# A new order of the boot in a two-layer memory-transformer kernel

## The chip, the cores and the metric

The kernel runs on one core of a Trainium2 chip. The metric is the device time of one execution in microseconds, the median of several runs. A core has five engines with instruction streams of their own: TensorE (PE, matrix products), VectorE (DVE), ScalarE (ACT), GpSimd (POOL) and SyncE (SP, which here only issues transfers). Transfers are started by an instruction on SP or POOL and then run by themselves.

## The reference

The input x is 2048 rows of 512 values in bfloat16. The reference does the same two steps twice, with the same weights:

```
x = x + A(layernorm(x))      # attention over segments, with a memory
x = x + B(layernorm(x))      # (sigmoid(x Wg) * (x Wu)) Wd, 512 -> 1792 -> 512
```

A cuts the 2048 rows into 64 segments of 32. For each segment, 8 memory rows are put ahead of the 32 rows, and 32 heads of width 128 attend over these 40 rows:

```
h = concat([mem, xs])                 # 40 x 512
q, k, v = h Wq, h Wk, h Wv            # 32 heads x 128
p = softmax(where(mask, q k^T * scale, -1e9))
o = (p v) Wo                          # 40 x 512
mem = o[:8]; out = o[8:]
```

The memory rows that come out of a segment go into the next, so the 64 segments of one layer are a chain; a segment can't begin its attention ahead of the end of the one before.

## The kernel before, in words

**Stages.** The first layer runs segment after segment, and the second follows six segments behind, so that most of the 70 steps (`NSTEPS`) work on one segment of each layer at once. A step (`emit_step`, L777) goes through five groups of heads, g0 to g4. For each part of a group it projects q and k (L874, from `hT`, the transposed normalised rows, with `wq_sb` and `wk_sb`), copies them from PSUM into `qku`, forms the scores (L910), adds the mask and takes the maximum on VectorE (L924 and after), the exponentials on ScalarE (L934), transposes the probabilities (L956), multiplies them with V (L982, `vsb`) and applies Wo (L1001). After every four segments a feed-forward block of 128 rows runs (`ffn`, L1056), whose weights POOL fetches anew every time (L1095, L1096, L1120).

**The boot.** V of the 32 plain rows of a segment doesn't depend on the memory, so V of the first layer is made in bulk in the boot: `v_group` and `v_pass` (L708, L631; matmuls L641) normalise 16 blocks of x, multiply them with `wv_sb`, and store the rows in a buffer in device memory, `scr`. `v_half` (L668) and `v_strip` (L698) do so for the parts that steps need first, with the matmuls at L768. From `scr` each step's V rows come back into `vsb` (L1230). Nine tiles of the feed-forward weights (`wd`, `wg`, `wu`) serve as staging for these stores until the first feed-forward block needs them; a staging tile is free once its store has landed. The strips have a single staging tile of their own, `sst`. Wv, Wq, Wk and Wo are loaded once (`load_weights`, L511, loads at L519): Wv in 8 loads of 4 heads, Wq and Wk in 6 loads each, of 3, 6 or 7 heads (384, 768 and 896 KB), Wo in 12.

**What sets the order.** The code names tasks with what they read and write (`Planner.add`): 13976 in all. The order in which the tasks are issued is not computed but stored: `SEQUENCE` (L53) is a compressed list with the place of each task among those still left, and behind it one bit for each task that may go on either of two engines (copies on ScalarE or VectorE, some transfers on SP or POOL). `plan` (L247) unpacks it. Each engine runs its tasks in this order, and a task waits for the tasks it depends on, so a task that waits holds up all behind it on its engine. Which PSUM bank or staging tile a task gets also follows from the order.

`replay` (L266) goes through the order once with the constants of L182 to L192 (rate of the transfers, times to landing and so on) and gives each task a planned start. The planned starts have two uses in the program. A large weight load on POOL is made to wait for a certain matmul, the last one that is planned to be done by the load's planned time:

```
w = (tk.nb + self.FIX) / self.CP
own = max(own, a) + w
t = max(t, own - self.LEAD[e] - self.ROOM)
tk.pace = pes[k].idx if k >= 0 else None
```

And `warm` (L340) puts matmuls without a purpose of their own (L1220) into planned pauses of TensorE.

## Time and profile before

| | |
|---|---|
| median of 3 runs | 1744.15 us |
| lowest and highest | 1743.08 and 1746.82 us |
| profiled execution | 1744.94 us |
| its span in the trace | 1743.2 us |
| TensorE busy in the span | 1718.3 us (99%) |
| VectorE, ScalarE, POOL busy | 1253.1, 1146.2, 872.6 us |
| bytes moved by transfers | 273.41 MB, 157 GB/s over the span |

A row of the timeline has the start, the time taken, engine, line and operation, the tile written and the tile read, and in the last bracket how long the engine had been idle before it and what ended the wait. A window row has the busy time of each engine in a stretch (with the number of instructions), the granted clock of TensorE as a share of full speed, the busy share of the 16 transfer engines and the rate. SPq and POOLq stand for the issuing of transfers on SP and POOL. A row of waits has the total, the number of times and the longest.

### The profile page before, as it was taken

The page shows a single profiled execution, that of the slowest core. Times are in us where ns is not written, and L with a number is a line of the kernel's source. Part 1 is how long each engine was busy: PE and PEld are TensorE (multiplying, and loading weights), DVE is VectorE, ACT ScalarE, POOL GpSimd, SP SyncE. Part 2 cuts the span into 40 slices and gives each one's busy share as a digit, 9 for nine tenths or more (in the row PEclk, how much of TensorE's full clock was granted, in tenths as well). Part 3 has the DMA queues.
Part 4 walks back from the last instruction along what each step waited for, and adds up shares of the span by engine and source line. Part 5 has one row for each costly group of instructions (what it writes and reads, how often), then busy time and mean ns, then how long its engine had stood idle before and what let it go on. Part 6 is the DMA issues. An engine that isn't in the chain of part 4 may idle for free.

```text
span 1743.2 us, 91561 instructions
## 1 busy us (share of the span) xinstructions
PE 1718.3 (99%) x38936; PEld 1492.0 (86%) x39151; DVE 1253.1 (72%) x4178; ACT 1146.2 (66%) x3149; POOL 872.6 (50%) x1401
## 2 busy tenths in 40 slices
PE   9899999999999999999999999999999999999999
PEld 4688789889898988989898888988888898988887
DVE  5677687677776766776677778776777876776766
ACT  4576777566666766676666666666666666666665
POOL 7535255545544564545455454645545454554443
PEclk9999999999999999999999999999999999999999
DMA  9835364655545464646455464545645454554544
GB/s 323 289 112 162 88 175 138 176 148 157 152 129 174 130 186 122 176 115 185 141 152 173 131 178 121 169 131 166 172 133 171 132 160 124 164 158 133 157 145 124
DMA packets 145155, 273.41 MB, mean 157 GB/s; under 512 B 39838, under 2 KB 86114, under 8 KB 144746
## 3 DMA queue, kind: packets, MB, share of 16 engines
q0 software_dynamic: 74144, 201.30, 39.7%
q1 hardware_dynamic: 70602, 66.25, 12.8%
q8 instruction: 307, 5.03, 1.2%
q14 instruction: 102, 0.84, 0.2%
HBM read 221.78 MB, written 27.07 MB: 143 GB/s over the span
## 4 chain that ended last, share of the span: by engine, by line
PE 91%; DVE 3%; DMA 2%; issue 1%; ACT 1%; SPq 0%; POOL 0%; DVEq 0%; POOLq 0%; ACTq 0%
PE bank L874 32%; PE bank L1001 17%; PE bank L1103 11%; PE bank L768 7%; PE bank L641 7%; PE bank L910 4%; PE bank L982 4%; PE bank L1126 4%; PE bank L956 2%; PE bank L601 1%; DVE st L924 1%; DMA wq_sb<-in_A_Wq_dram 1%; PE bank L1220 1%; DMA wk_sb<-in_A_Wk_dram 1%; PE bank L1071 0%
## 5 line engine op out<-in xcount | busy, mean ns | idle before, releaser
L874 PE MATMUL bank<-hT,wk_sb 128*128 128x80 bf16 (+3 forms) x8960 | 616.9, 198 | 3.5 <-DMA wk_sb<-in_A_Wk_dram 3.2
L874 PE MATMUL bank<-hT,wq_sb 128*128 128x80 bf16 (+3 forms) x8960 | 617.0, 198 | 2.2 <-DVE hT L1014 0.3
L1234 ACT CAST qku<-bank 128x480 bf16<-128x480 f32 (+3 forms) x770 | 384.1, 507 | 206.8 <-PE bank L874 179.2
L874 PEld LDWEIGHTS <-wq_sb 128*128 128x128 bf16 x8960 | 454.4, 99 | 31.8 <-issue 15.8
L874 PEld LDWEIGHTS <-wk_sb 128*128 128x128 bf16 x8960 | 447.5, 99 | 3.5 <-DMA wk_sb<-in_A_Wk_dram 3.5
L1001 PE MATMUL bank<-otsb,wo_sb 128*128 128x80 bf16 (+1 forms) x8960 | 355.7, 198 | 0.5
L924 DVE TENSOR_TENSOR st<-bank,cst 40x240 f32<-40x240 f32 (+3 forms) x768 | 280.9, 368 | 97.8 <-PE bank L910 81.8
L1001 PEld LDWEIGHTS <-wo_sb 128*128 128x128 bf16 x8960 | 333.3, 99 | 10.8 <-issue 0.6
L1230 POOL DMA_DIRECT2D vsb<-sst x360 | 182.3, 510 | 193.7 <-ACT sst L1234 86.9
L1234 ACT CAST otsb<-bank 128x480 bf16<-128x480 f32 (+3 forms) x420 | 200.4, 483 | 80.8 <-PE bank L982 47.1
L1120 POOL DMA_DIRECT2D wd<-in_B_w_down_dram x217 | 157.2, 725 | 136.3 <-PE bank L910 36.5
L1095 POOL DMA_DIRECT2D wg<-in_B_w_gate_dram x217 | 165.9, 765 | 118.3 <-PE bank L1103 53.2
L1096 POOL DMA_DIRECT2D wu<-in_B_w_up_dram x217 | 166.2, 767 | 106.0 <-PE bank L1103 36.2
L934 ACT ACTIVATE st<-st 80x240 f32<-80x240 f32 (+3 forms) x420 | 160.2, 383 | 73.1 <-DVE st L931 69.3
L1226 ACT ACTIVATE ptsb<-bank,small 120x160 bf16<-120x160 bf16 (+3 forms) x442 | 163.1, 387 | 16.0 <-PE bank L956 9.8
L1103 PE MATMUL bank<-xnT,wg 128*128 128x128 bf16 (+2 forms) x1784 | 171.4, 218 | 0.4
L936 DVE TENSOR_REDUCE small<-st 80x6 f32<-80x240 f32 (+3 forms) x420 | 151.7, 363 | 27.2 <-ACT st L934 25.0
L1103 PE MATMUL bank<-xnT,wu 128*128 128x128 bf16 (+2 forms) x1784 | 171.1, 218 | 0.0
L1230 POOL DMA_DIRECT2D vsb<-scr x197 | 104.4, 531 | 116.0 <-PE bank L982 57.0
L910 PE MATMUL bank<-qku 128*128 128x80 bf16 (+1 forms) x2240 | 159.3, 198 | 2.2 <-ACT qku L1234 0.9
L931 DVE TENSOR_TENSOR st<-st,small 80x240 f32<-80x240 f32 (+3 forms) x420 | 155.5, 371 | 7.8
L945 DVE TENSOR_TENSOR pb<-st,small 80x240 bf16<-80x240 f32 (+3 forms) x420 | 154.5, 370 | 7.4
(108 smaller groups left out, 2563.7 us busy)
## 6 DMA issues: line engine op xcount, KB each, us to landing
wg<-in_B_w_gate_dram POOLq DMA_DIRECT2D x220, 256.0 KB, 4.0
wu<-in_B_w_up_dram POOLq DMA_DIRECT2D x220, 256.0 KB, 4.1
wd<-in_B_w_down_dram POOLq DMA_DIRECT2D x220, 256.0 KB, 3.9
scr<-vst SPq DMA_DIRECT2D x90, 96.0 KB
vsb<-scr SPq DMA_DIRECT2D x120, 66.0 KB
vsb<-scr POOLq DMA_DIRECT2D x110, 66.0 KB, 3.2
vsb<-sst SPq DMA_DIRECT2D x189, 32.0 KB
vsb<-sst POOLq DMA_DIRECT2D x159, 32.0 KB, 2.5
```

The source lines that it names most:

```text
L874: nc.tensor.matmul(o_ap, lhsT=W[:, c, h * P:(h + 1) * P], rhs=mv(c), start=(c == 0), stop=(c == DC - 1))
L910: nc.tensor.matmul(s_all(SB)[:, w0 + i, :], lhsT=fview(qku[:, i, 0, 0:1], [(1, P)]), rhs=qku[:, i, 1, 0:ncol], start=True, stop=True)
L924: pl.add("DVE", dve_ns(n, True), lambda gsz=gsz, hs=hs, st=st, SB=SB, pj_=pj_, npj_=npj_, mk=mk, idx=idx: nc.vector.tensor_tensor(out=st[p ...
L934: pl.add("ACT", act_ns(n), lambda hs=hs, st=st: nc.scalar.activation(out=st[pr, hs], in_=st[pr, hs], func=ACTF.Exp, scale=self.scale), r=s ...
L1001: nc.tensor.matmul(WB[:, c * ncol:(c + 1) * ncol], lhsT=self.wo[:, h, c * P:(c + 1) * P], rhs=otsb[:, hl, 0:ncol], start=(h == 0 and c == ...
L1095: pl.add("POOL", 760, lambda wg=wg, fs=fs: nc.gpsimd.dma_start(out=wg[:], in_=self.wgv[:, :, fs]), r=[("wo", self.H - 1)], w=[gk] + bt, la ...
L1096: pl.add("POOL", 760, lambda wu=wu, fs=fs: nc.gpsimd.dma_start(out=wu[:], in_=self.wuv[:, :, fs]), r=[("wo", self.H - 1)], w=[uk] + bt, la ...
L1103: nc.tensor.matmul(gu[:, 2 * i + k, 0:n], lhsT=W[:, c, i * P:(i + 1) * P], rhs=xnT[:, c, rw], start=(c == 0), stop=(c == DC - 1))
L1120: pl.add("POOL", 760, lambda wd=wd, ip=ip: nc.gpsimd.dma_start(out=wd[:], in_=self.wdv[:, 2 * ip:2 * ip + 2, :]), w=[dk] + (["boot"] if se ...
L1226: nc.scalar.activation(out=dst, in_=src, func=ACTF.Copy, scale=by)
L1230: {"SP": nc.sync, "POOL": nc.gpsimd}[tk.on].dma_start(out=got[1], in_=got[2])
L1234: nc.scalar.copy(out=dst, in_=src)
```

## The change

`SEQUENCE` is replaced, and four constants of `replay` get other values: BUS from 330 to 322, TAIL from 1850 to 1900, STEAL from 1.2 to 0.5 and FIX from 12400 to 6000. The tasks themselves, their number and what they depend on stay as they are.

Unpacked, the two orders differ as follows. TensorE's tasks are in another order from the 8th to the 459th, which ended before at about 205 us; all later ones are the same. On ScalarE and VectorE some 400 and 440 tasks from the boot on are affected, on POOL the first 178 and on SP the first 180. 176 tasks change engine: on balance ScalarE gives 10 copies to VectorE, and SP and POOL exchange the same number of transfers. Some of the moves, with places counted from 0 in the order of the engine, and KB counted as the planner weighs the transfers up to and with the one named:

| | before | after |
|---|---|---|
| SP: Wo heads 16-18 (384 KB) | place 21 | place 55 |
| SP: Wq heads 3-8 | place 51 | place 39 |
| SP: Wk heads 9-15 | place 34, 9029 KB | place 41, 11296 KB |
| SP: Wk heads 25-31 | place 42, 11880 KB | place 47, 12272 KB |
| SP: Wk heads 19-24 | place 49, 13540 KB | place 50, 13840 KB |
| SP: Wk heads 3-8 | place 52, 15092 KB | place 52, 14614 KB |
| SP: last strip store | place 41, 10984 KB | place 38, 9603 KB |
| SP: last Wo load | 19007 KB | 18796 KB |
| POOL: one load of V rows of step 0 | place 72 | place 42 |
| three loads of V rows of step 0 | SP | POOL, places 50, 52, 59 |

On TensorE the projections of heads 28-30 and of 19-21 of the first step come later in the order, by the work of 3.75 and 4.6 us; those of heads 16-18 come earlier. The diff, with the packed text cut:

```diff
@@ -51,94 +51,94 @@
 
 
 SEQUENCE = r"""
-;BKuiQ(XWB|Nq;%M=J-2{;kc6bhnm~Jf#udN<eQ^8+sliGe<%`2z-?!iQne&XHLPcev^Yh%)*>c1|I@}$c!oj+)>wmhF5l(bm7~PF!TaafMXg-)GyJqkSJ?rI|_uaKd;QMmJ`D6B&P#NfhAGVGyKbnHoO*ebG?{r!^GC#GL~Pk-#;5
...
+;BKuidR+hrfBqEo|4vn>p;khd{li*ZCXwghSe{&(=4h=5NCmr+Y#L`tPw^|I?R@=@NHxH4-NR`(=ASRi2Z^+;LqX=pT}u32H0fZxYAZy8C-&EGSFzQV19<K#wCe8c-=?25UhOOLZ5LGGRes{0%jKSz72>O>qnn}mz%UbK<?nVyW=*`
...
@@ -185,8 +185,8 @@
     LAT = {"PE": 205.0, "DVE": 110.0, "ACT": 128.0, "POOL": 40.0, "SP": 4000.0}
     TO_PE, TO_POOL, PACE = 32.0, 257.0, 465.0
     WAIT = 65.0
-    BUS, BUS0, SLOW, BIG, ROOM, TAIL = 330.0, 304.0, 20400.0, 300000, 1.0, 1850.0
-    TAILP, CP, STEAL, FIX = 1000.0, 142.0, 1.2, 12400.0
+    BUS, BUS0, SLOW, BIG, ROOM, TAIL = 322.0, 304.0, 20400.0, 300000, 1.0, 1900.0
+    TAILP, CP, STEAL, FIX = 1000.0, 142.0, 0.5, 6000.0
     LEAD = {"SP": 600.0, "POOL": 2800.0}
     FIRST = {"PE": 0.0, "ACT": 2040.0, "DVE": 980.0, "POOL": 3500.0, "SP": 750.0}
     SPAN, COLD, WARM0, BACK = 3413.0, 4400.0, 1000.0, 2300.0
```

More of the change, by code (lines that the diff above doesn't have):

```diff
@@ new lines @@
+2P@>gl3pcm)&>P^4p770ETRdaIR!#8L6Y%L2cqSY93f-QmD;JbI1wav&$ITt^|;1NJmMq<nE1&t#6u$l-+h0(s}6PC&SIZZyNt!XyI_<;XJ2gNas0`5#&ZZbm_@p;#glZ38eph!2HZQmUEZ9>J$V61^=U_qA)$?5;&#y~N<g^U@wu@
+;k68_;M*TlG%b{bYWd|i=(-bjyh<Ibd;nieTyCB!mNfClp1-_`re_!rQw{WBV>g^g*k%(vY6qs6KrNfXRrmUw~3a9b&qj#k{YL9kLK>dU@qOu&mF<hTfRvhJ@bHm`_nJx`nPnm<;%O}Pk4JzJn`dRsXTIuNAf_!Y%1Eu>eQ=ScL#<B
+iT<fhQL3K)ImfRNLLrQfC-bN3cxlCFDj5jfLt!7Y)b^Q(DLZ0UkYqczF%9<Bq3Bl_W1q8HJ|9dJG;2A9Vmn1U>wScOB$|ZjBspV<f0@1-@poi7`}j1B-AW5uAUvo71llAA0{I*l%C)@e8}Tg{+Yi>JAO4*gJ=NFm+@~ErwRdpjU3M;
@@ new lines @@
+_KV1>ctfvA!SzuvKSTXOoua#XKbLYWv8=8+QQQ%8PkgQEE3a<$<F&Lg-tq?@_`z5YqD|}?-#((`z0MN-^0XwYp!h&_qt?dW>iO8_0hdqK8ArFGZ-EWt_rj<;KPyK1vhJ*<H<X<@5p~2u#$>GkkiK)V3+|BMlUB|FvJFQd-f9E2!;=w
+aQO%|<1(wnJOS$`rXM))TJ|8%_&pI>DbMPS)~iz^jFlMowUv9Ys2h<Q%KROWAPm)Yc7Eb!E4-GVgx$z(iGRSz9v8YWmo3zoW2BwML2GvU4WM!Va)EZleykT|SJLR<4fbhhTR-AQq6vB6k1CnNy0ohLQH$~QpDmd)7$;F(!2`Li@ZO{
+)1D8fIQ83d!V<>8cBejuZ4n)ODif83a|5<<eWgArAEd@CDqMy>P(El+)~2EpGw8>7O2#*&e_Wr@a85u!=TN`Y<rsep&OjCUDs+G4D^a!Np9fK@Yn6{=wQ5zkgxuCx>qd*BD2(m$io29a2}U8#w(3*Y=t|n9X^nqT2_blaWwE5E6)>L
@@ L142 @@
+XZFxZUFYixthDiwx#LRKU;{L<Dy_BY$^LEMqM?GTQtw$-k#^LJs-EbnhVX(j2J000
 """
```

169 lines of the change are left out of this document (81 added, 88 removed).

## The prediction

> **What bounds the kernel now.** I read the page first, for the engine that has no slack and for the part of the run where that is not so.
>
> ```profile
> span 1743.2 us, 91561 instructions
> PE 1718.3 (99%) x38936; PEld 1492.0 (86%) x39151; DVE 1253.1 (72%) x4178; ACT 1146.2 (66%) x3149; POOL 872.6 (50%) x1401
> PE   9899999999999999999999999999999999999999
> DMA  9835364655545464646455464545645454554544
> GB/s 323 289 112 162 88 175 138 176 148 157 152 129 174 130 186 122 176 115 185 141 152 173 131 178 121 169 131 166 172 133 171 132 160 124 164 158 133 157 145 124
> ```
>
> TensorE works 1718.3 us of 1743.2. All it leaves is 24.9 us, and no order can win more than that. Only the second slice (44 to 87 us) is below 9, and the first two slices are those in which the transfer engines are busy (9 and 8) and move 323 and 289 GB/s. So the boot, in which the weights come in, is where an order of the boot can matter. The windows say how much lies there (PE, PEld, DVE, ACT, POOL busy; then granted clock, transfer share, GB/s):
>
> ```profile
> 0.00:8.00 8.00, 6.94 (x30) 3.03 (x30) 4.02 (x14) 1.31 (x2) 6.15 (x26) 1.00 0.73 224
> 8.00:20.00 12.00, 11.80 (x67) 5.75 (x67) 7.94 (x24) 7.03 (x17) 5.13 (x14) 1.00 1.09 355
> 20.00:40.00 20.00, 19.50 (x159) 9.12 (x162) 12.86 (x35) 8.74 (x20) 17.28 (x33) 1.00 0.99 330
> 40.00:60.00 20.00, 15.72 (x258) 9.88 (x260) 9.71 (x23) 7.95 (x22) 13.79 (x27) 0.99 1.06 380
> 60.00:80.00 20.00, 19.77 (x365) 14.30 (x367) 11.91 (x39) 11.55 (x37) 8.16 (x16) 0.92 0.82 272
> 220.00:420.00 200.00, 198.42 (x4556) 176.41 (x4582) 150.35 (x514) 138.56 (x380) 108.29 (x173) 1.00 0.55 158
> ```
>
> From 8 to 60 us TensorE idles 0.20 + 0.50 + 4.28 = 4.98 us, 4.28 of it from 40 to 60 us, where the transfer share is 1.06: saturated. Past 220 us it idles 1.58 us in 200, with nothing left to win. Its own rows name each idle stretch (last bracket: idle time before, and what ended it):
>
> ```profile
> 25.83 1.47 PE L641 MATMUL bank<-wv_sb,xvf 128*128 128x512 bf16 x6 [0.34 <-ACT xvf L1234]
> 44.56 0.27 PE L874 MATMUL bank<-hT,wq_sb 128*128 128x54 bf16 x4
> 46.35 0.24 PE L910 MATMUL bank<-qku 128*128 128x40 bf16 x3 [0.94 <-ACT qku L1234]
> 47.44 0.27 PE L874 MATMUL bank<-hT,wk_sb 128*128 128x54 bf16 x4 [0.51 <-DMA wk_sb<-in_A_Wk_dram]
> 52.85 0.27 PE L874 MATMUL bank<-hT,wk_sb 128*128 128x54 bf16 x4 [0.77 <-DMA wk_sb<-in_A_Wk_dram]
> 59.38 0.28 PE L874 MATMUL bank<-hT,wk_sb 128*128 128x54 bf16 x4 [1.90 <-DMA wk_sb<-in_A_Wk_dram]
> ```
>
> Three are landings of Wk: heads 25-31 at 47.44, heads 19-24 at 52.85, heads 3-8 at 59.38. The 0.94 is one step removed: ScalarE's copy of the q/k tile stood behind a copy into the single strip staging tile `sst`, whose last store had not landed.
>
> ```profile
> 45.06 0.59 ACT L1234 CAST sst<-bank 128x512 bf16<-128x512 f32 x1 [2.94 <-DMA scr<-sst]
> ```
>
> After the last wait the granted clock falls to half:
>
> ```profile
> 44.00:47.40 3.40, 1.99 (x50) 1.32 (x42) 1.63 (x5) 1.70 (x5) 3.37 (x7) 1.00 1.06 399
> 56.00:59.40 3.40, 1.44 (x16) 0.88 (x16) 2.63 (x6) 1.77 (x5) 1.60 (x3) 1.00 1.09 337
> 59.75:63.17 3.42, 3.42 (x87) 3.42 (x83) 0.80 (x2) 1.25 (x5) 3.11 (x6) 0.50 0.99 335
> 60.30 1.80 PE bank L874 x40
> 80.27 0.61 PE bank L874 x24
> ```
>
> The last two rows, of the chain of waits, price the half clock: 45 ns a projection matmul in the cold stretch, 25 ns at 80 us. The same 3.42 us of work at 25/45 of the time would take 1.9, so the cold stretch costs 1.5 us. 1.96 us idle in 3.4 was enough to cool; 1.41 in 3.4 (44 to 47.4) was not. The Trainium skill ("TensorE: Matmul & The Clock Gate", Part 1) says instead that the clock halves after at least one idle window of about 3.4 us. This trace disagrees, with a wait of 1.90 us; by the page's rule no wait of this size would cost clock, and 1.5 us of the gain below would have to be found elsewhere.
>
> **The change, part by part.** No instruction is added or removed: the same 13976 tasks run in another order. TensorE's first 452 tasks are reordered (the first 7 and all after some 205 us stay as they are), some 400 tasks of ScalarE, 440 of VectorE, 180 of SP and 178 of POOL. So the sum is of waits, and each is followed by the queue that ends it.
>
> *Rate of the queue.* The weights go out on SP, and how many KB the order issues up to a load can be counted. Before, it is 11880 up to Wk 25-31 and 15092 up to Wk 3-8; they landed at 47.44 and 59.38. SP's transfers thus land at 3212 / 11.94 = 269 KB/us. If POOL's vanished from the stretch, SP would get at most the whole 380 GB/s, 371 KB/us.
>
> ```profile
> wk_sb<-in_A_Wk_dram SPq DMA_DIRECT2D x2, 896.0 KB
> wk_sb<-in_A_Wk_dram SPq DMA_DIRECT2D x2, 768.0 KB
> wo_sb<-in_A_Wo_dram SPq DMA_DIRECT2D x10, 384.0 KB
> 49.78 0.37 SPq L519 DMA_DIRECT2D wk_sb<-in_A_Wk_dram  x1
> SPq L519 <- DMA wq_sb<-in_A_Wq_dram: 3.0, 2, 1.8
> ```
>
> *Wo 16-18 goes behind all Wq and Wk* (SP position 21 to 55), and some smaller transfers with it, while others come ahead: the count up to Wk 3-8 falls from 15092 to 14614, by 478 KB. That is 1.78 us sooner at 269 KB/us, 1.29 at 371; I take the middle, 1.53, so the load lands at 57.85 (57.6 to 58.1). It stays at SP's position 52, and 49.78 was its issue; weight issues on SP wait for landings (the last row), so it comes earlier if the loads ahead land earlier. If not, this term is nil.
>
> *TensorE's order.* Up to Wk 3-8 the new order puts 0.83 us more work ahead of it (counted by the durations of the same instructions). So TensorE comes to that load 1.53 us sooner and has 0.83 us more behind it: 2.36 us of the 4.98 are won, 2.62 remain. The waits at 47.44 and 52.85 go because the projections of heads 28-30 and 19-21 are placed 3.75 and 4.6 us later among TensorE's work, while their loads land only 1.46 and 1.1 us later (392 and 300 KB more ahead, at 269).
>
> *What is late instead.* Wk 9-15 moves back from 9029 to 11296 KB, 584 KB ahead of where Wk 25-31 stood: it lands 1.57 to 2.17 us ahead of 47.44, at 45.3 to 45.9. TensorE needs it for heads 9-11, before at 44.56, now with 0.80 us less ahead and the 0.34 of 25.83 perhaps saved: 43.4 to 43.8. A new wait of 1.5 to 2.4 us stands there, and the one at Wk 3-8 shrinks to what is left of 2.62. If the new wait cools the clock, 1.5 us are lost, but they are lost ahead of the landing at 57.85, where TensorE would have waited some 0.8 us anyway: net 0.7 us. If it does not, nothing cools, and the 1.5 us of 59.75 are saved whole. I take it as saved (1.5; bounds 0.8 and 1.5).
>
> *Strip stores and `sst`.* The last strip store goes from SP position 41 to 38 (10984 to 9603 KB), 1381 KB or 3.7 to 5.1 us sooner, so the 2.94 us wait of ScalarE shrinks to nothing, and the 0.94 with it. That is inside the 4.98 already and isn't counted twice.
>
> *POOL.* Four loads of step 0's V rows stand earlier among POOL's instructions (one from position 72 to 42, three come over from SP at 50, 52, 59), and each waits for strip stores; queued behind them are the stores that empty the nine boot staging tiles, and behind these VectorE's copies into those tiles. The nearest rows:
>
> ```profile
> POOL vsb L1230 <- DMA scr<-sst: 5.3, 2, 4.5
> 68.63 0.52 POOL L1230 DMA_DIRECT2D scr<-wd  x1 [5.48 <-ACT kx L1234]
> ```
>
> Two such waits before held 5.3 us, 4.5 at most. By the earlier stores they should find the data landed (strip stores at 9603 KB, against 9029 KB for a load that before was in use by TensorE at 44.56). Price between 0 and 4.5; nearest is the small one (5.3 less 4.5 is 0.8). What of that reaches TensorE through VectorE, which is busy 9.7 of 20 us from 40 to 60, I take as 0.3.
>
> *The rest.* 176 copies and transfers change engine, 10 net from ScalarE to VectorE, some 0.5 us each: covered by ScalarE's and VectorE's idle half from 40 to 60 us; if that cover went, ScalarE's copies of q/k would be late by 0.5 each. The last Wo load falls from 19007 to 18796 KB, 0.8 us sooner at 269, while TensorE is 3.5 us sooner: Wo was first used at 72.57, and the output projections may wait up to 1.5 us; the order has them later, so I take none. The constants (BUS, TAIL, STEAL, FIX) reach the chip only through which matmul a paced weight load on POOL waits for: (370000 + 12400) / 142 becomes (370000 + 6000) / 142, 45 ns per load; and through the filling matmuls (L1220), which stand in pauses. I cost it at nothing: such a load has 4.0 us to landing and TensorE's idle past 220 us is 0.8% whatever they do. Later waits of the boot are kept as they are, with 0.7 either way:
>
> ```profile
> 72.57 0.46 PE L1001 MATMUL bank<-otsb,wo_sb 128*128 128x40 bf16 x12
> wg<-in_B_w_gate_dram POOLq DMA_DIRECT2D x220, 256.0 KB, 4.0
> 153.97 0.83 PE L768 MATMUL bank<-wv_sb,hT 128*32 128x512 bf16 x12 [0.47 <-issue]
> 186.87 0.53 PE L982 MATMUL bank<-ptsb,vsb 120*128 120x120 bf16 x7 [0.67 <-DMA vsb<-sst]
> ```
>
> **Sum.** 2.36 (waits) + 1.5 (clock) - 0.3 (POOL) = 3.56 us. The profiled execution was 1744.94 us with a span of 1743.2, so 1741.4 for its like; the median of the runs is 0.8 below it, and from 1744.15 it is 1740.6.
>
> The Trainium skill ("DMA: Bandwidth & Descriptors", "Issuing engines are not separate DMA queues") says that transfers of all issuing engines interleave on the same 16 and that spreading the issues saves only the issue time. The share of 1.06 agrees. Read strictly it speaks against this change, and gives the first rival.
>
> **Rivals.**
> - *The queue gives it back.* SP's 478 KB only change places with POOL's bytes: up to 59.38 the same total lands, 380 GB/s in both, and Wk 3-8 still lands at about 59.3. Then TensorE idles 4.98 less 0.83, the clock cools as before, and 1744.15 - 0.83 gives 1743.3. For it: the share is already full, and three loads go from SP to POOL. Against: POOL issues no more than before up to there, and 384 KB do move behind. The counterpart, that the order doesn't matter at all, gives 1744.15.
> - *Slower: POOL's queue stands.* If the moved V-row loads wait as long as the 5.48 of the row above, the staging tiles stay full, VectorE's copies stand, and the softmax behind them on VectorE with them; TensorE then has nothing but landed projections. One wait of 5.48 and a second of 1.5, less 0.5 of slack, are 6.5 at TensorE, and the clock cools for 1.5 more: 1740.6 + 6.5 + 1.5 = 1748.6. It is a loss from 2.1 us at TensorE on, and one of 0.2% from 5.5. For it: the boot has only nine staging tiles, and POOL waited 5.48 once. Against: the stores they wait for are sooner.
> - *Everything goes.* The new wait is small since POOL is behind and SP gets up to 371 KB/us: 4.98 less 1.0, and the clock, and nothing at POOL: 1744.15 - 4.0 - 1.5 = 1738.6.
>
> **How the numbers follow.** Forecast 0.40, queue 0.28, POOL 0.20, everything 0.12. No change, for a measurement of this kernel, is within 0.2% or 3.5 us: 1740.7 to 1747.6. The forecast lies at that edge, so its chance splits, 0.28 faster and 0.12 same; with 0.12 of the last that makes 0.40 faster. The queue case is same, but for 0.04 that is slower, should the new wait for Wk 9-15 come on top; of POOL's, 0.15 are slower. Faster 0.40, same 0.41, slower 0.19. The forecast's own range is 1739.3 (all bounds good, 58.1 to 57.6 and no loss at POOL, 0.7 at the later waits) to 1742.7 (1.29 for 1.53, 0.8 for 1.5, 0.8 at POOL, 0.7 later). Over all cases 1738.4 to 1748.0 leaves out 1 in 10 on the slow side and less on the fast.
>
> **What would show it.** Wk 3-8's first matmul at 57.6 to 58.1 less any earlier start; no row with 0.94 behind ScalarE; a new wait of 1.5 to 2.4 us for Wk 9-15 at 45 to 46; granted clock at 1.00 from 60 to 80; idle from 8 to 60 of about 2.6. Wrong, if Wk 3-8 lands at 59 or later (the queue), if TensorE waits for VectorE or ScalarE past 60 us with POOL standing for `scr<-sst` (POOL's queue), or if idle grows past 220 us, where the order is the same.

## The result and the profile after

| | before | after |
|---|---|---|
| median of 18 runs each, taken together on one chip | 1745.61 us (1742.61 to 1747.92) | 1748.89 us (1746.77 to 1752.21) |
| ratio | | 1.0022, 95% interval 1.0015 to 1.0029 |
| profiled execution | 1744.94 us, span 1743.2 | 1750.46 us, span 1748.7 |

The new order is slower: by 3.8 us going by the ratio (0.0022 of 1745.6), by 3.3 us going by the medians. The prediction said 1740.6, with a chance of 0.40 for faster, 0.41 for the same and 0.19 for slower; its forecast is wrong in sign. The two profiled executions lie 5.5 us apart.

The page of the changed kernel: span, busy times, and TensorE in 40 slices.

```profile
span 1748.7 us, 91578 instructions
PE 1720.0 (98%) x38938; PEld 1491.7 (85%) x39153; DVE 1257.5 (72%) x4188; ACT 1139.7 (65%) x3139; POOL 871.6 (50%) x1401
PE   9999999999999999999999999999999999999998
```

The page alone would mislead: the second slice (44 to 87 us) has gone from 8 to 9 for TensorE, as if the boot had become better. TensorE's busy time is up by 1.7 us with two more matmuls; 1.15 of it are filling matmuls (L1220) in the boot, which do no work of the kernel. The windows are clearer. First the kernel before, in stretches that were not shown (PE, PEld, DVE, ACT, POOL busy; then granted clock, transfer share, GB/s):

```profile
8.00:60.00 52.00, 47.01 (x481) 24.75 (x488) 30.51 (x82) 23.72 (x58) 36.20 (x72) 1.00 1.04 355
110.00:140.00 30.00, 29.76 (x908) 25.74 (x906) 23.53 (x82) 21.11 (x79) 9.31 (x15) 1.00 0.35 93
180.00:206.00 26.00, 25.17 (x617) 21.16 (x612) 17.95 (x68) 20.71 (x60) 7.64 (x14) 1.00 0.34 96
```

The windows of the changed kernel:

```profile
8.00:60.00 52.00, 48.72 (x506) 25.58 (x510) 30.72 (x86) 23.43 (x56) 34.91 (x67) 1.00 1.02 341
60.00:80.00 20.00, 17.27 (x273) 10.88 (x273) 13.36 (x42) 9.07 (x27) 10.15 (x19) 0.91 0.92 302
110.00:140.00 30.00, 29.14 (x898) 25.20 (x896) 21.01 (x76) 20.22 (x75) 8.32 (x14) 1.00 0.37 105
180.00:206.00 26.00, 24.11 (x564) 19.53 (x565) 17.96 (x64) 17.77 (x50) 6.92 (x13) 1.00 0.33 87
```

From 8 to 60 us TensorE idles 3.28 us instead of 4.99: that is 1.71 us less idle time, where 2.36 were predicted. Even of that only some 0.6 us went into work, for the filling matmuls take 1.47 us of this stretch instead of 0.32. In the repeats below the new order gets less work done there than the old (46.23 us for 47.20). From 60 to 80 us it idles 2.73 instead of 0.23, which loses 2.50 at once; the granted clock of that stretch is as low as before (0.91 for 0.92). Two later stretches lose 0.62 and 1.06; the first of these is one wait of 0.69 at 116.73 for which the profile names nothing. That adds up to 2.47 us more idle, and TensorE's rows name most of it. The last row is a task from which on both orders are the same, so it can mark the end of the boot. The timeline of TensorE in the changed kernel (last bracket: idle time before, and what ended it):

```profile
11.61 0.40 PE L601 MATMUL bank<-cst,xn 128*128 128x128 bf16 x4 [0.84 <-DVE xn L592]
42.08 1.05 PE L768 MATMUL bank<-wv_sb,hT 128*32 128x512 bf16 x16 [0.76 <-ACT qku L1234]
50.05 0.27 PE L874 MATMUL bank<-hT,wk_sb 128*128 128x54 bf16 x4 [0.18 <-DMA wk_sb<-in_A_Wk_dram]
54.91 0.26 PE L874 MATMUL bank<-hT,wq_sb 128*128 128x54 bf16 x4 [0.80 <-DVE wg L1236]
59.45 0.26 PE L874 MATMUL bank<-hT,wq_sb 128*128 128x54 bf16 x4
62.57 0.26 PE L874 MATMUL bank<-hT,wq_sb 128*128 128x54 bf16 x4 [2.36 <-DVE wd L1236]
190.23 0.53 PE L982 MATMUL bank<-ptsb,vsb 120*128 120x120 bf16 x7 [1.68 <-DMA vsb<-sst]
212.57 0.59 PE L1001 MATMUL bank<-otsb,wo_sb 128*128 128x80 bf16 x12
```

The same last row in the kernel before:

```profile
209.20 0.59 PE L1001 MATMUL bank<-otsb,wo_sb 128*128 128x80 bf16 x12
```

The waits for weights are gone but for 0.18 us: heads 3-5, the first to use Wk 3-8, begin at 59.45 without any. In their place TensorE waits for copies, on VectorE and once on ScalarE: 0.84, 0.76, 0.80, 2.36. The boot ends at 212.57 instead of 209.20, 3.37 us later, and what comes behind it, in the same order, takes 2.1 us more. The timed loss is 3.8.

Why VectorE is late is on its own rows of the changed kernel's timeline:

```profile
9.84 1.71 DVE L592 TENSOR_SCALAR xn<-xs,small 128x512 bf16<-128x512 bf16 x1 [0.44 <-POOL small L591]
40.75 0.41 DVE L592 TENSOR_SCALAR xn<-xa,small 128x512 bf16<-128x512 bf16 x1 [4.18 <-POOL small L591]
54.16 0.69 DVE L1236 CAST wg<-bank 128x512 bf16<-128x512 f32 x1 [3.31 <-PE bank L910]
61.83 1.29 DVE L1236 CAST wd<-bank 128x512 bf16<-128x512 f32 x2 [3.44 <-DMA scr<-wd]
```

and on POOL's:

```profile
9.76 0.77 POOL L505 MEMSET pb<- 80x384 bf16 x2
10.91 1.07 POOL L509 MEMSET qku<- 128x480 bf16 x2
39.61 0.52 POOL L1230 DMA_DIRECT2D vsb<-scr  x1 [1.08 <-DMA scr<-sst]
47.51 0.51 POOL L1230 DMA_DIRECT2D scr<-wg  x1 [0.46 <-DMA scr<-wu]
54.32 0.53 POOL L1230 DMA_DIRECT2D vsb<-scr  x1 [1.61 <-DMA scr<-wg]
55.64 1.03 POOL L1230 DMA_DIRECT2D scr<-wd  x2
```

The operation of 9.84 in the kernel before:

```profile
9.88 0.46 DVE L592 TENSOR_SCALAR xn<-xs,small 128x512 bf16<-128x512 bf16 x1 [0.44 <-POOL small L591]
```

There are three causes, in order of time.
- At 9.84 a VectorE operation takes 1.71 us that took 0.46 before, while POOL fills memory from 9.76 to 11.98. TensorE waits 0.84 for its result.
- At 39.61 a V-row load that was moved up waits on POOL for a strip store to land. A small operation of the layer norm (L591) stands behind it, VectorE idles 4.18 us for that, and TensorE 0.76 for what VectorE makes.
- At 61.83 VectorE's copy waits for its staging tile to be empty. The store that empties it went out on POOL at 55.64 and took 6 us to land. It stands on POOL behind a V-row load that waited 1.61 us at 54.32. At 54.16 another copy waits in the same way: its store went out at 47.51, and the idle time of 3.31 ends as it lands, though the row names a matmul that had been done for long.

The chain of waits of the changed kernel runs through the last of these:

```profile
55.64 5.97 DMA scr<-wd
...
62.57 0.77 PE bank L874 x24
```

So it is the second rival of the prediction ("POOL's queue stands"), which forecast 1748.6 with 0.20 of the chance, but with another last link. That rival's staging tiles stay full because V-row loads on POOL wait for strip stores, with the other stores behind them. That happens here, but with waits of 1.08 and 1.61 us where the rival took 5.48; the larger part is that the stores themselves stand late in the order and land slowly. That its 1748.6 comes so near the measured 1748.89 is luck, since it was added up from waits that the rows don't show. Counted from the issue rows, the stores of the boot issued by 48 us are 3672 KB before and 3048 KB after, and the weights issued by then 11264 and 12416 KB.

The transfers as a whole also ran slower. Windows of the kernel before and of the changed one:

```profile
36.00:52.00 16.00, 14.39 (x238) 8.78 (x239) 7.88 (x19) 5.87 (x16) 11.83 (x23) 1.00 1.05 387
36.00:52.00 16.00, 14.79 (x219) 8.79 (x222) 9.12 (x26) 5.92 (x15) 12.11 (x23) 1.00 0.96 320
```

The transfer records show what that did to Wk 3-8, the load on which the prediction's first term rests. SP issues it at 47.81 instead of 49.78, and 465 KB less of SP's and 404 KB less of POOL's have landed ahead of it, but its last packet lands at 58.37 instead of 58.45. That SP and POOL stood on waits, so that fewer transfers were under way, is a likely reason; no run here shows it.

### The profile page after: what moved, and what is told of

It reads as the page before. It is cut to its first block, busy times and chain, and to the rows that moved or that the text cites. A ratio compares the mean times of both kernels' runs of the same rounds, so it can differ in the third digit from the quotient of the medians.

```text
span 1748.7 us, 91578 instructions
## 1 busy us (share of the span) xinstructions
PE 1720.0 (98%) x38938; PEld 1491.7 (85%) x39153; DVE 1257.5 (72%) x4188; ACT 1139.7 (65%) x3139; POOL 871.6 (50%) x1401
## 4 chain that ended last, share of the span: by engine, by line
PE 91%; DVE 4%; DMA 2%; ACT 1%; issue 1%; POOL 0%; SPq 0%; DVEq 0%; ACTq 0%; POOLq 0%
PE bank L874 32%; PE bank L1001 17%; PE bank L1103 11%; PE bank L768 7%; PE bank L641 7%; PE bank L910 4%; PE bank L982 4%; PE bank L1126 4%; PE bank L956 2%; DVE st L924 1%; PE bank L601 1%; DMA wq_sb<-in_A_Wq_dram 1%; PE bank L1220 1%; PE bank L1071 0%; DVE small L929 0%
## 5 line engine op out<-in xcount | busy, mean ns | idle before, releaser
L1226 ACT ACTIVATE ptsb<-bank,small 120x160 bf16<-120x160 bf16 (+4 forms) x440 | 161.7, 385 | 17.7 <-PE bank L956 11.5
```

The lines of the kernel that those rows point to most:

```text
L1226: nc.scalar.activation(out=dst, in_=src, func=ACTF.Copy, scale=by)
```

## The experiments

An edit changes places in an order, so the diffs below are lists of instructions of one engine in the order of issue: line, operation, tile written and tile read, shape. Each group of kernels ran with its own runs of the kernel before on the same chip. The end of the boot is read from the row shown above. Filling matmuls (L1220) come and go with the planned pauses in some of them, up to 13 matmuls; where a kernel leaves them out, it is said.

**One store up (e2).** The store behind the wait at 61.83 goes from POOL's place 73 to 59, right behind the store that shares its tile's name:

```diff
POOL
 L1230 DMACopy scr_60<-wg_122 16x2x384
-L1230 DMACopy scr_60<-wd_129 16x4x384
+L1230 DMACopy scr_60<-wd_129 16x4x384 x2
 L1230 DMACopy vsb_80<-scr_60 8x1024
...
 L1230 DMACopy vsb_80<-sst_120 32x1024
-L1230 DMACopy scr_60<-wd_129 16x4x384
```

> The changed order with only the store of place 73 moved up to place 59. Theory 1: the wait of 2.36 us and the half clock go, and the one of 0.80 at 54.91 stays or grows by up to 0.6 (the store it waits for comes one transfer later): 3 to 3.9 us faster than the changed kernel, about 1745.5. Theory 2: unchanged within 1 us.

Measured: 1749.31 us against 1748.48 for before, ratio 1.0008 (0.9996 to 1.0020); the boot ends at 208.76. The timeline of e2, rows of POOL, VectorE, ScalarE and TensorE:

```profile
42.04 1.05 POOL L1230 DMA_DIRECT2D scr<-wd  x2
...
58.67 1.29 DVE L1236 CAST wd<-bank 128x512 bf16<-128x512 f32 x2 [0.58 <-PE bank L641]
69.52 1.07 ACT L1234 CAST wg<-bank 128x512 bf16<-128x512 f32 x2 [3.21 <-DMA scr<-wg]
70.16 0.25 PE L956 MATMUL bank<-cst,pb 66*128 66x66 bf16 x3 [2.34 <-ACT wg L1234]
```

Both stores now go out by 43.09, the second without a wait, so its tile was ready at least 12 us before it went out in the changed kernel. The wait at 61.83 is gone (0.58 at 58.67, for a matmul): the store's late place caused it. The copy of 54.16 still waits, now 4.03 us at 53.74. A wait of the same size stands 8 us later, for the next tile: ScalarE's copy waits 3.21 for a store, and TensorE 2.34. The kernel is no longer measurably slower than before, nor is it faster; its interval overlaps that of the change itself (1.0015 to 1.0029).

**Two stores up (e1).** The same, and the store behind the copy at 54.16 from POOL's place 63 to 55. That one takes its tile free earlier, so two later copies swap staging tiles:

```diff
VectorE
-L1236 TensorCopy wu_124<-bank_139 128x512
+L1236 TensorCopy wg_121<-bank_139 128x512
 L1236 TensorCopy kx<-bank_138 128x84
-L1236 TensorCopy wg_121<-bank_140 128x512
+L1236 TensorCopy wu_124<-bank_140 128x512
```

> The changed order, with two stores of boot staging tiles moved up on POOL: the one that VectorE's copy at 61.83 waited for (place 73, issued at 55.64) goes to place 59, behind the first store of the same tile, and the one that VectorE's copy at 54.16 waited for (place 63, issued at 47.51) goes to place 55. Theory 1 (single late stores hold a staging tile and with it all of VectorE): both waits of VectorE (3.44 and 3.31 us) fall below 1 us, TensorE's waits of 2.36 and 0.80 us go, nothing halves the clock at 63 us; the time falls by 2.4 + 0.8 + 1.5 = 4.7 us if nothing else is late, to about 1744.2 from 1748.9, at least by 3. Theory 2 (the transfer queue is full, and a store that is moved up only makes another one late): VectorE waits for the next staging tile instead, TensorE idles as long from 40 to 80 us (4.75 us) and the time stays at 1748.9 within 1 us. Theory 3 (the constants, through which matmul a weight load waits for): no change, as they are the same here.

Measured: 1752.14 against 1748.48, 1.0027 (1.0014 to 1.0040), and the boot ends at 213.76. It is no better than the change itself. VectorE's two waits for staging tiles, of 3.31 and 3.44 us, are gone in its trace, and TensorE waits 1.92 at 70.66 for a ScalarE copy instead, and 1.54 where it waited 0.76 at 42.08.

**The constants alone (e3).** The new order with the old constants; the program then differs from the changed kernel by two and a quarter filling matmuls.

```diff
-    BUS, BUS0, SLOW, BIG, ROOM, TAIL = 322.0, 304.0, 20400.0, 300000, 1.0, 1900.0
-    TAILP, CP, STEAL, FIX = 1000.0, 142.0, 0.5, 6000.0
+    BUS, BUS0, SLOW, BIG, ROOM, TAIL = 330.0, 304.0, 20400.0, 300000, 1.0, 1850.0
+    TAILP, CP, STEAL, FIX = 1000.0, 142.0, 1.2, 12400.0
```

> The changed order with the four constants of before. The program differs from the changed kernel by 2 1/4 more filling matmuls at 50.6 us and by nothing else, no weight load waits for another matmul. Theories 1 and 2: 1748.9, at most 0.5 more for the filling (2.25 x 0.21 us). Theory 3 (the constants cost the time): back to 1745.6.

Measured: 1752.37 against 1748.48, 1.0021 (1.0008 to 1.0034). The loss is the order's, and the constants cost nothing that these runs can show, as predicted. Its profiled execution is still one of the quick ones (span 1744.7, boot end 209.30), with the same wait, but the granted clock stays at 1.00 behind it. A row of TensorE's timeline in e3:

```profile
61.77 0.26 PE L874 MATMUL bank<-hT,wq_sb 128*128 128x54 bf16 x4 [2.25 <-DVE wd L1236]
```

**Wo behind Wk, alone (e4).** The part of the change on which the prediction's first term rests, made in the kernel before:

```diff
SP
 L519 DMACopy wo_sb<-in_A_Wo_dram 128x512
-L519 DMACopy wo_sb<-in_A_Wo_dram 128x3x512
 L730 DMACopy oxT_1_104<-in_A_x_dram 128x512
...
 L519 DMACopy wk_sb<-in_A_Wk_dram 128x4x768
+L519 DMACopy wo_sb<-in_A_Wo_dram 128x3x512
 L1230 DMACopy vsb_81<-scr_60 8x384
```

> The kernel before, with the load of Wo heads 16-18 (384 KB) alone moved on SP behind the load of Wk heads 3-8. The step of the prediction on the queue's rate: 384 KB / 269 KB/us = 1.43 us, so Wk 3-8 lands at 57.95 in place of 59.38, the earlier Wk landings at 47.44 and 52.85 come as much earlier and TensorE idles 1.4 less from 40 to 60 us; the wait at 59.38 falls below what halves the clock (1.5 more): 1.4 to 2.9 us faster, 1742.7 to 1744.2 for 1745.6. The first rival (the queue gives it back): Wk 3-8 lands at 59 or later, no change within 0.5 us.

Measured: 1749.77 against 1748.48, 1.0009 (0.9998 to 1.0020). Wk 3-8 is used from 58.81, where two executions of before have 59.38 and 58.87. TensorE's timeline in e4:

```profile
58.81 0.27 PE L874 MATMUL bank<-hT,wk_sb 128*128 128x54 bf16 x4 [1.39 <-DMA wk_sb<-in_A_Wk_dram]
```

384 KB less ahead on SP should have been 384 / 269 = 1.43 us by the prediction's rate. What came is 0.06 to 0.57, in one execution. The rate at which a queue delivers was not the price of the KB taken out of it. Two things bear on why. SP issued the load no earlier (49.70, and 49.78 and 49.63 in before), the case for which the prediction had called its term nil. And the place left free wasn't taken by POOL: by 58.81 it had moved 3623 KB, and 3622 and 3623 in before. Rather the transfers ran slower, at 312 GB/s from 20 to 36 us where the two executions of before have 322 and 341.

**Weights first (g3).** The same, and five small transfers of SP (92 KB) behind Wk 3-8 as well, so that what stands ahead of it is 14616 KB, as in the changed kernel:

```diff
SP
 L519 DMACopy wq_sb<-in_A_Wq_dram 128x4x768
+L519 DMACopy wk_sb<-in_A_Wk_dram 128x4x768
+L519 DMACopy wq_sb<-in_A_Wq_dram 128x4x768
+L519 DMACopy wk_sb<-in_A_Wk_dram 128x4x768
+L519 DMACopy wo_sb<-in_A_Wo_dram 128x3x512
 L1230 DMACopy scr_60<-wg_123 8x4x256
 L1230 DMACopy scr_60<-wg_123 8x4x384
 L1230 DMACopy vsb_80<-scr_60 8x256
 L1230 DMACopy scr_60<-wd_128 16x4x256
-L519 DMACopy wk_sb<-in_A_Wk_dram 128x4x768
 L1230 DMACopy scr_60<-wu_124 8x4x256
-L519 DMACopy wq_sb<-in_A_Wq_dram 128x4x768
-L519 DMACopy wk_sb<-in_A_Wk_dram 128x4x768
```

> The kernel before with only the weights on SP put forward: Wo heads 16-18 and five small transfers of the boot (92 KB) behind the load of Wk heads 3-8; 14616 KB up to that load in place of 15092, as in the changed kernel, and the order on every other engine as before. The step of the prediction (478 KB are 1.3 to 1.8 us): Wk 3-8 lands at 57.6 to 58.1, TensorE idles 1.5 less from 40 to 60 us. Theory A adds: no staging tile is late by this, as the stores moved are small, so the gain stays: 1.5 us faster, and more where the clock is not halved. Theory B: Wk 3-8 lands at 59 or later, or a wait of the same size at a staging tile or a V row takes its place; no change within 0.7 us.

Measured: 1748.75 against 1747.01, 1.0005 (0.9996 to 1.0014). TensorE's timeline in g3:

```profile
58.50 0.28 PE L874 MATMUL bank<-hT,wk_sb 128*128 128x54 bf16 x4 [0.25 <-DMA wk_sb<-in_A_Wk_dram]
73.20 0.47 PE L1001 MATMUL bank<-otsb,wo_sb 128*128 128x40 bf16 x12 [1.55 <-DMA wo_sb<-in_A_Wo_dram]
```

Even 476 KB, with the load issued at 44.32, move Wk 3-8 by only 0.4 to 0.9 us. What is won there (0.25 us of wait for 1.90 or 1.51) is paid back at the first uses of Wo, 1.55 at 73.20 and 1.59 at 77.31.

**Stores off POOL (f1).** e2, and two more stores (192 and 64 KB) go from POOL to SP, ahead of the Wo loads:

```diff
POOL
 L1230 DMACopy scr_60<-wd_127 8x4x384
-L1230 DMACopy scr_60<-wg_123 96x1024
...
 L591 TensorTensor small<-small,cst 128x1
-L1230 DMACopy scr_60<-wg_123 8x4x1024
SP
 L1230 DMACopy scr_60<-wu_125 16x2x1024
+L1230 DMACopy scr_60<-wg_123 96x1024
+L1230 DMACopy scr_60<-wg_123 8x4x1024
 L519 DMACopy wo_sb<-in_A_Wo_dram 128x3x512 x2
```

> The changed order with the store of POOL's place 73 at place 59, and the two stores (192 and 64 KB) of the staging tile that ScalarE waited for in the run before (e2: 3.21 us at 69.52, which held TensorE 2.34 us at 70.16) given from POOL (places 80 and 84) to SP, directly ahead of the eight Wo loads that SP issues from 57 to 66 us. Filling matmuls as in the changed kernel. Theory A (the staging tiles as a whole drain too slowly, because the weights on SP were put ahead of stores, and the first tile that is late is where TensorE stands): with these two out of the way the wait at 70 falls below 0.5 us, and as POOL issues two stores fewer the ones behind come 1.1 us earlier; TensorE idles less than 2 us from 60 to 80, the time is 2 to 4 us below the changed kernel on the same chip. Theory B (the queue is full whatever the order, each move makes another store late): a wait of 2 us or more stands at yet another tile or at a Wo load, and the time is that of the changed kernel within 1.5 us.

**All up (f2).** f1, and the store at POOL's place 63 directly behind the first one of its tile; two staging tiles swap as in e1.

```diff
VectorE
-L1236 TensorCopy wu_124<-bank_139 128x512
+L1236 TensorCopy wg_121<-bank_139 128x512
```

> The same as the one before, and the store of POOL's place 63 right behind the first store of its tile as well. Theory A: VectorE's wait at 53.7 (4.0 us) falls to about 1.3 as it did with the two stores moved up together, and 0.5 us more are won at most, as TensorE didn't stand there. Theory B: no faster than the changed kernel.

Measured: f1 1750.41 against 1747.01, 1.0018 (1.0010 to 1.0027); f2 1748.80, 1.0016 (1.0007 to 1.0025). The boots end at 208.92 and 208.00. TensorE's largest wait from 50 to 75 us is 1.62 in f1 (at 55.48, for VectorE's copy into `wg`) and 1.27 in f2 (at 65.48, for ScalarE's copy into `wg`).

The profiled boots are 3.7 and 4.6 us shorter than that of the changed kernel, and TensorE's waits of 2 us and more are gone. In the time of the runs less of it shows: the medians are 1.5 and 3.1 us below that of the changed kernel on the same chip (h below), and the intervals overlap. That ends of boots alone don't settle the time is seen from the repeats that follow.

**Both kernels again (h, i).** No edit; two more profiles of the same programs show what one program does from execution to execution.

> The changed kernel, as it is, on the chip of these three: the reference for the first two. The waits of VectorE at 54 and 62 us stand again (3 us each, within 0.5), and TensorE's wait of 2.3 at 62. All theories: 0.2% slower than before. If the clock is halved by chance, it is at 1.00 here or at 0.91 from 60 to 80 us as in the first trace, with a difference of 1.5 us.

> The kernel before, as it is: a second trace of it, on the chip of the next two. Its boot (up to the first task from which both orders are the same, 209.20 us in the first trace) holds the waits for Wk at 47, 53 and 59 us again, in all 3 us within 1; whether the clock is halved after the last is open. If it is not, the boot ends 1.5 us sooner, near 207.7.

Measured: after again 1751.91 against 1747.01, 1.0032 (1.0015 to 1.0048); before again 1744.03 against 1745.41, 0.9993 (0.9983 to 1.0003), no difference. TensorE's timeline in after again, and then the window:

```profile
63.19 0.26 PE L874 MATMUL bank<-hT,wq_sb 128*128 128x54 bf16 x4 [2.04 <-DVE wd L1236]
212.87 0.59 PE L1001 MATMUL bank<-otsb,wo_sb 128*128 128x80 bf16 x12
```

```profile
60.00:80.00 20.00, 17.50 (x316) 11.64 (x316) 13.46 (x43) 9.48 (x28) 10.44 (x20) 1.00 0.99 327
```

The same of before again:

```profile
58.87 0.28 PE L874 MATMUL bank<-hT,wk_sb 128*128 128x54 bf16 x4 [1.51 <-DMA wk_sb<-in_A_Wk_dram]
206.46 0.59 PE L1001 MATMUL bank<-otsb,wo_sb 128*128 128x80 bf16 x12
```

```profile
60.00:80.00 20.00, 19.77 (x412) 14.16 (x415) 12.82 (x42) 12.47 (x40) 10.14 (x20) 1.00 0.85 286
```

The waits are properties of the order: the one on `wd` is there in all three executions of the new order (2.36, 2.25, 2.04), and 60 to 80 us loses 2.27 us here too (17.50 for 19.77). The end of the boot varies by 3 us for one order: 212.57, 212.87 and, with the old constants, 209.30 for the new one; 209.20 and 206.46 for the old one, and 206.79 in e4, whose edit is small. The means are 211.6 and 207.5, 4.1 apart, which is the size of the timed loss. With g3, also a small edit of before, whose boot ends at 210.89, the difference is 3.2. What lies behind the end of the boot took 1534.0 and 1534.3 us in the two traces of before, 1536.1 and 1537.3 in the two of after, and from 1534.9 to 1543.6 (e4) in the other eleven, with almost the same instructions in the same order. In e4 a wait of 1.71 us for V rows at 526.37 and half the clock behind it make up 3.75 us of it; in the other traces most of the difference lies in the last 110 us. Why it is there is open.

**POOL tidied (j1).** In the changed kernel, the fills of `pb`, `ptsb` and `qku` no longer stand beside the VectorE operation of 9.84, and the small operation of 40.15 goes ahead of the two V-row loads:

```diff
POOL
 L503 Memset hT_70 128x4x40
-L591 TensorTensor small<-small,cst 128x1
 L505 Memset pb_85 80x384
 L505 Memset pb_86 80x384
 L507 Memset ptsb_88 128x480
+L591 TensorTensor small<-small,cst 128x1 x2
 L509 Memset qku_77 128x480
 L509 Memset qku_78 128x480
-L591 TensorTensor small<-small,cst 128x1
...
 L1230 DMACopy scr_60<-wu_126 16x4x1024
+L591 TensorTensor small<-small,cst 128x1
 L1230 DMACopy vsb_80<-scr_60 8x256
 L1230 DMACopy scr_60<-wg_122 16x2x1024
 L1230 DMACopy vsb_81<-scr_60 8x384
-L591 TensorTensor small<-small,cst 128x1
```

> The changed order with POOL alone put in another order, at two places ahead of 45 us. (1) The five fills of memory that POOL does from 9.76 to 11.98 us go elsewhere (three into its idle time ahead of 9.16, two behind the next small operation). If they are what makes VectorE's operation at 9.84 take 1.71 us where its like take 0.41, it takes 0.5 or less now and TensorE's wait of 0.84 at 11.6 goes; if not, both stay. (2) The small operation of the layernorm that VectorE waited for (4.2 us, to 40.75) goes ahead of the two loads of V rows that waited for strip stores (1.1 to 1.9 us each). If these loads are the cause, VectorE goes on at about 38.3 and TensorE's wait at 42 us (0.34 to 1.63) goes. Staging tiles: the waits at 54 and 62 us stand, and take back what was won ahead of them, as they end with a store: TensorE's wait at 62 grows from 2.0-2.4 to as much as 4. The time: no more than 1 us faster than the changed kernel (1.0032 of before on the last chip, 1.0022 on the first).

Measured: 1749.29 against 1745.41, 1.0015 (1.0006 to 1.0024), boot end 213.57. The timeline of j1, VectorE and then TensorE:

```profile
10.12 0.41 DVE L592 TENSOR_SCALAR xn<-xs,small 128x512 bf16<-128x512 bf16 x1 [0.45 <-POOL small L591]
38.59 0.41 DVE L592 TENSOR_SCALAR xn<-xa,small 128x512 bf16<-128x512 bf16 x1 [1.71 <-POOL small L591]
47.24 0.27 PE L874 MATMUL bank<-hT,wk_sb 128*128 128x54 bf16 x4 [1.60 <-DMA wk_sb<-in_A_Wk_dram]
```

Both causes are shown: the operation takes 0.41 us without the fills, and VectorE goes on at 38.59 instead of 40.75. TensorE's waits of 0.84 and 0.76 go. What they gave is taken back at 47.24, where heads 9-11 now wait 1.60 us for Wk 9-15, and in new waits of 0.43 at 9.73 and 0.65 at 21.03. The wait at 47.24 is the one that the prediction had forecast (1.5 to 2.4). In the changed kernel it was 0.12, which fits TensorE's coming later there. But 1.60 is one execution: in j2 (next), which makes the same two moves, it is 0.19.

**All of it (j2).** j1 with f2, two small stores (29 and 19 KB) further up, and the filling matmuls at 50.6 left out:

```diff
TensorE
-L1220 Matmult bank_140<-hot 128x512
-L1220 Ldweights hot
-L1220 Matmult bank_140<-hot 128x512
...
```

> All that was found, in one: POOL as in j1, the stores moved as in f2, two more small stores of a staging tile (29 and 19 KB, on which ScalarE waited 2.46 us in f2) behind their like at place 58, and the four filling matmuls at 50.6 us left out. Theory A (single late stores and two misplaced steps of POOL make up the loss): no wait of TensorE over 0.7 us ahead of 140 us, the boot ends at 206 to 207 us (208.0 in f2, less 0.7 at 11 us, 1.3 at 65 and 0.8 of filling, of which some comes back as a wait for weights), and the time is that of before within 1 us, or below it. Theory B (the queue is full, what is won at one place is lost at the next): the boot ends at 208 or later and the time stays 1.5 us or more above before.

Measured: 1749.43 against 1745.41, 1.0023 (1.0014 to 1.0032), boot end 209.92. A row of the chain of waits of j2, and then two of its timeline:

```profile
52.48 6.51 DMA scr<-wu
```

```profile
59.14 0.59 ACT L1234 CAST wu<-bank 128x512 bf16<-128x512 f32 x1 [5.14 <-DMA scr<-wu]
59.78 1.87 PE L641 MATMUL bank<-wv_sb,xvf 128*128 128x512 bf16 x4 [4.32 <-ACT wu L1234]
```

The moves pushed another store back, which goes out at 52.48 and takes 6.51 us to land; TensorE waits 4.32 us for it. That the stores that went up took the time of this one is likely and not shown.

**Wq 3-8 back (k1).** The change moved Wq 3-8 (768 KB) up on SP from place 51 to 39. It goes back, directly ahead of Wk 3-8, with nothing else changed:

```diff
SP
 L705 DMACopy scr_60<-sst_120 8x4x1024 x2
-L519 DMACopy wq_sb<-in_A_Wq_dram 128x4x768
 L1230 DMACopy scr_60<-wg_122 16x2x384
...
 L519 DMACopy wk_sb<-in_A_Wk_dram 128x4x768
+L519 DMACopy wq_sb<-in_A_Wq_dram 128x4x768
 L1230 DMACopy vsb_81<-scr_60 8x384
 L519 DMACopy wk_sb<-in_A_Wk_dram 128x4x768
```

> The changed order with one weight load put back: Wq heads 3-8 (768 KB), which the change had moved up to SP's place 39 although its first use is at 59 us, goes back directly ahead of Wk heads 3-8; nothing else changes. Theory A (weights put too far ahead of their use take the queue from the stores of the staging tiles; SP and POOL share one queue): the stores that POOL issues from 36 to 50 us land up to 768 KB / 350 KB/us = 2.2 us sooner, VectorE's waits at 54 and 62 us (3.3 and 3.4 us) shrink by 1 us or more each, TensorE's wait at 62 (2.0 to 2.4) falls below 1.2, and the boot ends at 211 or earlier (212.6 and 212.9 in the two traces of the changed kernel). Theory B (POOL's own stores in flight are the limit, whatever SP moves): the waits for staging tiles at 54 and 62 stand within 0.5 us, and the boot ends at 212 to 213.

Measured: 1748.00 against 1745.91, 1.0012 (1.0003 to 1.0020), boot end 209.25. The timeline of k1, VectorE and TensorE:

```profile
53.42 0.69 DVE L1236 CAST wg<-bank 128x512 bf16<-128x512 f32 x1 [1.51 <-DMA scr<-wg]
60.84 0.27 PE L874 MATMUL bank<-hT,wk_sb 128*128 128x54 bf16 x4 [1.38 <-DMA wk_sb<-in_A_Wk_dram]
61.46 1.29 DVE L1236 CAST wd<-bank 128x512 bf16<-128x512 f32 x2 [3.25 <-DMA scr<-wd]
```

768 KB of weights that no one needed yet were a part of the late stores: VectorE's wait at 54 falls from 3.31 and 3.17 (the two traces of the changed kernel) to 1.51, in one trace. The one at 61 stays (3.25), so that store is late for its place on POOL, as e2 shows by moving it. By the ratios about half of the loss is gone (0.0012 for 0.0022), but the two intervals overlap.

**Wq 3-8 back and stores up (k2).** k1 and f1 together, without the filling matmuls at 50.6:

```diff
SP
 L1230 DMACopy scr_60<-wu_125 16x2x1024
+L1230 DMACopy scr_60<-wg_123 96x1024
+L1230 DMACopy scr_60<-wg_123 8x4x1024
 L519 DMACopy wo_sb<-in_A_Wo_dram 128x3x512 x2
```

> The same, with the one late store moved up (place 73 to 59), the two stores of the next tile on SP (as in f1), and the filling matmuls at 50.6 us left out. Theory A: no wait at a staging tile over 1 us, the boot ends at 207 (208.9 in f1, less 0.8 filling and 1 or more at the waits that f1 still had, 1.62 at 55), and the time comes within 1.5 us of the kernel before. Theory B: a wait of 1.5 us or more at a staging tile stays, the boot ends at 208.5 or later, 2 us or more above before.

Measured: 1748.28 against 1745.91, 1.0013 (1.0002 to 1.0024), boot end 210.17. The wait of 61 is gone, that of 54 is 2.44 again, and ScalarE waits 2.21 at 69.1. No better than k1. None of the kernels beats the one before.

## Why the prediction was wrong, point by point

- **The bound.** Right: what the order changes is TensorE's waits in the boot. The end of the boot moved by 3.37 us in the two profiles and by 3.2 to 4.1 in the means, and the time by 3.8. The 24.9 us of slack and the 1.58 us idle past 220 are too much, though: the trace of before lacks 215 matmuls (38936 for 39151 weight loads), and the traces that lack none (e1 to e4) have 0.2 to 0.5 us idle from 220 to 420 us.
- **Rate of the queue (478 KB are 1.53 us).** This step failed: in the changed kernel Wk 3-8 landed 0.1 us sooner (last packet at 58.37 for 58.45), though it was issued 2 us earlier, and the repeats differ by more (59.59 in after again, 57.06 in e3, 58.26 in before again). 384 KB alone gave 0.06 to 0.57 us (e4), 476 KB gave 0.4 to 0.9 (g3). The step held the rate fixed, between 269 and 371 KB/us; in the changed kernel all transfers together fell from 387 to 320 GB/s from 36 to 52 us. The rival "the queue gives it back" had the landing right, but not its reason, the same total landed: it was less. The Trainium skill ("DMA: Bandwidth & Descriptors", "Issuing engines are not separate DMA queues") has all transfers interleave on the same 16 engines; that a landing hardly moved by its queue's own KB is in keeping with it.
- **TensorE's order.** Right: the waits at 47.44, 52.85 and 59.38 for weights went but for 0.18 us. But TensorE idled 1.71 us less up to 60 us, not 2.36, and 1.15 of that is filling matmuls.
- **The new wait for Wk 9-15 (1.5 to 2.4 us).** Such a wait can come: j1 shows it with 1.60; in the changed kernel it was 0.12, where TensorE had lost 0.84 and 0.76 us before it, and in j2 0.19.
- **`sst`.** Right: no row is left with 0.94 behind the strip's staging tile.
- **POOL (0.3 us).** This step failed too, and it decides the sign. It said that the V-row loads "should find the data landed". One waited 1.08 us, and the small operation behind it held VectorE for 4.18. More was lost by what the step didn't price at all: stores on POOL that empty staging tiles, late in their queue and 6 us in landing. At TensorE it comes to 0.76 + 0.80 + 2.36 = 3.92 us, against a bound of 4.5 that the step had itself taken from the rows. The working chose the row at the small end, on the ground that the strip stores were sooner; it didn't go through the nine staging tiles, each with its store's issue and landing, which is where the larger waits came from.
- **The fills on POOL.** Not seen in the prediction: five fills had moved beside a VectorE operation, which cost 0.84 us.
- **The clock (1.5 us saved).** Wrong in this profile: 0.91 from 60 to 80 us, for the 2.36 us wait. After again and e3 have the same wait and keep 1.00: where the wait falls counts too (below), and neither order is rid of it. Nor is it what makes the new order slower: 11 of its 18 runs have a mean granted clock of 1.000, and they take 1748.7 us in the mean, where all 18 of before take 1745.3.
- **Wo's waits, taken as none.** Right in the changed kernel: no row of TensorE waits for Wo in the boot. In g3, with Wo as late and TensorE not held up, they appear with 1.55 and 1.59, so the bound of 1.5 was a fair one for each.
- **Later waits (0.7 either way).** The one for V rows at 186.87 grew from 0.67 to 1.68, which is most of the 1.06 lost from 180 to 206. With the 0.62 between 110 and 140 the later stretches lose 1.68, where 0.7 was allowed.
- **Constants at nothing.** Right (e3).
- **The sum.** Forecast -3.56, measured +3.8. By the rows of the two profiles: waits won up to 60 us -1.71 (-2.36 forecast, and the 0.76, 0.80 and 0.84 are already in it), 60 to 80 us +2.50, later +1.68, clock 0 instead of -1.5. That makes 2.47 us, or 3.62 with the 1.15 of filling matmuls; the boot ended 3.37 us later. So three terms failed: POOL's 0.3 for 3.92, the rate's 1.53 for 0.1, and the clock's 1.5 for nothing.

What stays open: by how much each of the causes counts in the time of the runs. Variants without one or two of them lie between 1.0008 (e2) and 1.0027 (e1), and most of their intervals overlap; when a wait was removed, others mostly appeared elsewhere, and what lies behind the boot varies by more than the effect. In f1 TensorE has no wait of 2 us in the boot and all 11 runs have a clock of 1.000, and it's still slower (1.0018); so no variant shows that the three causes make up the whole timed loss.

## What to carry to other kernels

In a boot full of transfers it isn't enough to count the KB that stand ahead of the load that is waited for; ask too which transfers give way to it. Here these were stores that empty staging tiles, so list for each staging tile when it is full, when its store goes out, when that lands, and who writes the tile next. Take one move out and measure it alone before a rate is multiplied with KB: 384 KB that "should" be 1.43 us were 0.06 to 0.57. And when a wait is removed, look for the next one behind it that was hidden by being late, as the wait for Wk 9-15 may have been.

## What the runs showed of the hardware

- **A wait's length doesn't settle the clock; where it falls counts too.** Waits of 2.36 us (after) and 1.90 us (before) were followed by a granted clock of 0.91 and 0.92 from 60 to 80 us; waits of 2.25 us (e3) and 2.04 us (after again) left it at 1.00, as did 1.51 in before again. In each trace the changes of the granted clock lie whole multiples of 3.41 us apart, so each trace can be cut into pieces of 3.41 us. Where TensorE idled 1.95 us or more of a piece, the next was at half clock in every trace; up to 1.63 us it never was; from 1.65 to 1.86 both are seen. The pieces with the waits named, in after (2.13 us idle, cold behind it), after again (1.75) and e3, where the wait is split over two (1.44 and 0.81):

```profile
60.44:63.85 3.41, 1.28 (x51) 1.27 (x51) 1.76 (x4) 0.46 (x2) 2.02 (x4) 1.00 1.09 367
61.44:64.86 3.42, 1.67 (x58) 1.55 (x59) 2.16 (x6) 0.43 (x3) 2.87 (x6) 1.00 1.08 349
57.55:60.96 3.41, 1.97 (x52) 1.52 (x51) 0.43 (x2) 1.36 (x4) 1.51 (x4) 1.00 1.09 355
```

  So the prediction's figure, that 1.96 us idle in 3.4 is enough to cool, held on such pieces, but not for any 3.4 us. The Trainium skill ("TensorE: Matmul & The Clock Gate", Part 1) says that the window of 3413 ns runs freely. That agrees with the spacing; that a whole idle window is needed does not agree, as the piece idled 2.13 us in after and 2.49 in j2 (with its 4.32 us wait) and no more.
- **Filling memory on POOL holds up VectorE.** An operation of 0.46 us took 1.71 while POOL filled memory beside it from 9.76 to 11.98, and 0.41 with the fills away (j1). In before, two shorter fills (0.39 us for both, from 9.80) stood beside the same operation, and it took 0.46. The Trainium skill ("SBUF — State Buffer", "SBUF: two separate sides") describes a shared pair of ports that one of VectorE (in some modes) and GpSimd holds for a whole instruction while the other waits. That VectorE was held up agrees with it; that it was by these ports no run here shows.
- **A store takes some 6 us to land while the weights come in.** 5.97 us from issue for one of 48 KB (after) and 6.51 for another (j2), at a share of 1.06 to 1.08 meanwhile.
- **One program's boot ends up to 2.7 us apart** (206.46 and 209.20 in two executions of before), so one profile can't tell a change of 0.2%.
